# Transposing shifted attention scores by row halves of the PE array, and reordering the first token list of the routed MLP

## The chip, the cores and the metric

One core of one Trainium2 chip runs the kernel. The metric is the device time of one execution in microseconds (us); the kernel before took 655.96 us in the median of three runs (654.54 to 656.99).

## The reference

An attention with two kinds of local masks (heads 0 to 3: the last 32 keys; heads 4 to 7: every fourth of the last 128 keys) feeds a routed MLP with eight experts, in which every expert takes exactly `N // E` = 576 tokens, greedily by descending logit.

```python
q, k, v: (8, 8, 576, 64)   x: (4608, 512)   w1: (8, 512, 1024)   w2: (8, 1024, 512)
scores = scale * q @ k^T, masked;  attn = exp(scores - max) / (sum + 1e-9);  x = attn @ v
logits = x @ w_gate
for idx in argsort(-logits.flatten()):          # token idx // E, expert idx % E
    if assigned[tok] >= 0 or counts[e] >= cap: continue
    assigned[tok] = e; counts[e] += 1
for e: out[assigned == e] = relu(x[assigned == e] @ w1[e]) @ w2[e]
```

## The kernel before

The program has two stages, each with its own planner (class `Schedule`). The planner knows every operation's cost in ns, its dependencies and a boost to its due time; it simulates the engines and writes out a fixed order for each of them. An engine then executes its list in that order, whatever the real durations are. A matmul operation carries a form (how the PE array is divided); a change of form is planned at `T_TURN` = 95 ns.

**Attention.** There are 32 units (8 batches, two mask kinds, two head pairs of each kind). A unit handles two heads in nine blocks of 64 queries by 96 keys, ordered even blocks first (`ORD`, five even and four odd, `GR`). Its steps are: `scores` on PE (36 matmuls of 64x64 tiles of the array, form "quarter", into two PSUM banks `pm`); `most` on DVE (mask and row maximum, nine instructions); `shift` on POOL (subtract the maximum, one instruction for each of the two groups); `turn` on PE (nine transposes of [128 queries of two heads, 96 keys], form "whole", three to a PSUM bank `pS`, two banks in turn); `exps` on ACT (three instructions of 96x384); `values` on PE (36 matmuls, form "half", two groups into banks `px`); `sums` on ACT and `weigh` on DVE. After both head pairs of a kind, `banks` transposes the result on PE (nine transposes of 128x128, form "whole", three to a bank) and ACT copies it out; SP stores it to HBM (`xd`). Loads and stores share SP's queue in program order. `tokens` computes the gate logits, and `Router.choose` makes sort keys and the one-hot choice of each token on DVE (`keys`, `choices`).

**First list.** Between the stages, `Router.alone` runs with nothing beside it: a radix search over all keys (`search_alone`, PE and DVE in turn) finds the logit at which the first expert fills; then DVE finds which expert it is (`largest`, `expert`), its members (`members`), their ranks on PE (`ranks`), which of them are accepted (`need_of`, `accept`), their slots, digits and one-hot rows (`slots`, `digits`, `by_chunk` on POOL, `by_row` on ACT, `within` on DVE), and PE and DVE turn these into a list of row indices (`place`, `indices`). POOL gathers the tokens by that list with five indirect DMAs (`gather`).

**Experts.** Eight rounds of two matmul chains in split fp32r (high and low parts), while DVE searches for the next expert's list. `weights` casts the expert's weights on ACT (high part) and subtracts on DVE (low part).

PSUM is full: two banks `pm`, two `pS`, three `px` and one of the router.

## Time and profile before

| | us |
|---|---|
| median of three runs | 655.96 |
| the profiled execution | 656.71 |
| its span, first to last instruction | 654.7 |
| PE busy over the span | 619.2 (95%) |
| attention, to about | 158 |
| search of the first list, alone | 158 to 176 |
| first list and first gather | 176 to 193 |
| experts | 193 to 655 |

In a row of the profile a time is the start in us from the span's first instruction, followed by how long the instruction or the merged run of instructions took. Matmuls overlap, so the cost of one is read from start to start of the runs, not from its own duration. PEld is PE's weight load, SPq is SP's queue of DMA issues. A bracket at the end of a row is the idle time before it and what ended it.

### The profile page before, as it was taken

The page shows a single profiled execution, that of the slowest core. Times are in us where ns is not written, and L with a number is a line of the kernel's source. Part 1 is how long each engine was busy: PE and PEld are TensorE (multiplying, and loading weights), DVE is VectorE, ACT ScalarE, POOL GpSimd, SP SyncE. Part 2 cuts the span into 40 slices and gives each one's busy share as a digit, 9 for nine tenths or more (in the row PEclk, how much of TensorE's full clock was granted, in tenths as well). Part 3 has the DMA queues.
Part 4 walks back from the last instruction along what each step waited for, and adds up shares of the span by engine and source line. Part 5 has one row for each costly group of instructions (what it writes and reads, how often), then busy time and mean ns, then how long its engine had stood idle before and what let it go on. Part 6 is the DMA issues. An engine that isn't in the chain of part 4 may idle for free.

```text
span 654.7 us, 17735 instructions
## 1 busy us (share of the span) xinstructions
PE 619.2 (95%) x6635; PEld 534.3 (82%) x6636; DVE 454.1 (69%) x1916; ACT 306.9 (47%) x691; POOL 203.2 (31%) x322
## 2 busy tenths in 40 slices
PE   8999999997569999999999999999999999999994
PEld 5877788885439977987998898799889879989983
DVE  3768678875787888975897899689789927615200
ACT  3867788762038356742453434245344435324210
POOL 3434343330053167461025106202510621421011
PEclk9999999998579999999999999999999999999998
DMA  9999999623049379971154235115423643211010
GB/s 315 389 306 305 305 297 305 148 54 66 10 130 260 63 195 279 242 250 41 57 179 152 74 130 170 49 58 176 155 74 126 211 155 137 74 49 58 0 41 32
DMA packets 62646, 100.12 MB, mean 153 GB/s; under 512 B 7264, under 2 KB 26208, under 8 KB 62560
## 3 DMA queue, kind: packets, MB, share of 16 engines
q1 hardware_dynamic: 53216, 73.81, 34.6%
q0 software_dynamic: 9344, 25.17, 14.1%
q8 instruction: 52, 0.85, 0.5%
q14 instruction: 34, 0.28, 0.1%
HBM read 73.80 MB, written 18.87 MB: 142 GB/s over the span
## 4 chain that ended last, share of the span: by engine, by line
PE 70%; issue 12%; DVE 7%; POOL 4%; DMA 4%; ACT 1%; SPq 0%; POOLq 0%; DVEq 0%; ACTq 0%
PE ph L1207 26%; PE py L1249 17%; PE px L423 5%; PE pS L415 5%; PE pm L397 4%; PE px L474 2%; POOL xg L1155 2%; PE pz L657 2%; PE ptx L1170 2%; DMA xd<-xs 2%; POOL out L1275 2%; PE py L1252 1%; PE py L1254 1%; DVE ob L962 1%; PE pz L736 1%
## 5 line engine op out<-in xcount | busy, mean ns | idle before, releaser
L1249 PE MATMUL py<-w2h,hb 128*128 128x512 f32 x512 | 171.3, 399 | 0.0
L1207 PE MATMUL ph<-xh,w1h 128*128 128x256 f32 (+1 forms) x512 | 138.4, 301 | 0.7 <-ACT xh L1037 0.7
L1207 PE MATMUL ph<-xl,w1h 128*128 128x256 f32 (+1 forms) x512 | 136.3, 297 | 0.0
L1207 PE MATMUL ph<-xh,w1l 128*128 128x256 f32 (+1 forms) x512 | 136.2, 296 | 0.0
L1249 PEld LDWEIGHTS py<-w2h,hb 128*128 128x128 f32 x512 | 96.2, 188 | 18.9
L1037 ACT ACTIVATE hb<-ph 128x256 fp32r<-128x256 f32 (+2 forms) x192 | 59.8, 346 | 97.5 <-PE ph L1207 96.8
L1249 PE MATMUL py<-w2l,hb 128*128 128x512 f32 x256 | 100.0, 390 | 0.0
L1275 POOL DMA_INDIRECT out<-y,tok x40 | 41.0, 1025 | 169.0 <-ACT y L1037 95.8
L1207 PEld LDWEIGHTS ph<-xh,w1h 128*128 128x128 f32 x512 | 91.6, 190 | 1.4 <-ACT xh L1037 1.1
L1207 PEld LDWEIGHTS ph<-xh,w1l 128*128 128x128 f32 x512 | 91.6, 190 | 0.1
L1207 PEld LDWEIGHTS ph<-xl,w1h 128*128 128x128 f32 x512 | 91.4, 190 | 0.0
L408 POOL TENSOR_TENSOR sc<-sc,mx 128x480 f32<-128x480 f32 x64 | 56.9, 910 | 90.2 <-DVE mx L402 90.2
L1227 DVE SCALAR_TENSOR_TENSOR hb<-ph,hb 128x256 fp32r<-128x256 f32 (+1 forms) x128 | 57.3, 454 | 30.5 <-ACT hb L1037 28.7
L1037 ACT ACTIVATE y<-py 128x512 f32<-128x512 f32 (+1 forms) x40 | 23.9, 598 | 102.8 <-PE py L1249 95.4
L402 DVE CUSTOM_DVE_ANT_0 sc<-pm,const 128x96 f32<-128x96 f32 x288 | 53.8, 253 | 24.1 <-PE pm L397 24.0
L1155 POOL DMA_INDIRECT xg<-xd,idx x40 | 41.9, 1049 | 47.8 <-PE ph L1207 35.3
L1249 PEld LDWEIGHTS py<-w2l,hb 128*128 128x128 f32 x256 | 48.2, 188 | 8.4
L411 ACT ACTIVATE et<-pS 96x384 f32<-96x384 f32 x96 | 43.3, 485 | 23.9 <-PE pS L415 23.1
L1037 ACT ACTIVATE w1h<-raw 128x512 fp32r<-128x512 f32 x64 | 38.8, 629 | 28.1 <-DMA raw<-in_moe_w 27.2
L415 PE MATMUL pS<-const,sc 128*96 128x128 f32 x288 | 44.0, 281 | 1.0 <-ACT et L411 0.9
L1038 DVE TENSOR_TENSOR w2l<-raw,w2h 128x512 fp32r<-128x512 f32 x48 | 30.9, 685 | 19.1 <-ACT w2h L1037 18.8
L1037 ACT ACTIVATE xh<-ptx 128x512 fp32r<-128x512 f32 (+1 forms) x36 | 20.0, 555 | 51.4 <-PE ptx L1170 51.0
(170 smaller groups left out, 1024.4 us busy)
## 6 DMA issues: line engine op xcount, KB each, us to landing
raw<-in_moe_w SPq DMA_DIRECT2D x128, 256.0 KB, 5.1
k<-in_kp SPq DMA_DIRECT2D x16, 304.0 KB, 6.1
k<-in_kd SPq DMA_DIRECT2D x16, 304.0 KB, 6.4
q<-in_qp SPq DMA_DIRECT2D x16, 288.0 KB, 5.3
q<-in_qd SPq DMA_DIRECT2D x16, 288.0 KB, 6.2
xd<-xs SPq DMA_DIRECT2D x64, 72.0 KB, 2.9
xd<-xs SPq DMA_DIRECT2D x16, 288.0 KB, 6.2
w2l<-raw POOLq DMA_DIRECT2D x16, 256.0 KB, 5.5
```

Source lines behind the costliest of these rows:

```text
L402: nc.vector.tensor_tensor_reduce(out=sc[:, c], in0=pms[g][:, c // 2 * KB:c // 2 * KB + KB], in1=mm[:, c if self.kind else min(1, c)], scal ...
L408: nc.gpsimd.tensor_tensor(sc[:, g::2], sc[:, g::2], mx[:, g::2, None].to_broadcast([128, n, KB]), op=OP.subtract)
L411: nc.scalar.activation(self.E0[:, 384 * j:384 * j + 384], pt[:KB, :384], AF.Exp, scale=-1.0)
L415: nc.tensor.transpose(pt[:KB, 128 * x:128 * x + 128], sc[:, ORD[3 * j + x]], C["identf"])
L423: nc.tensor.matmul(px[64 * a:64 * a + 64, x - c0], self.E0[:, w:w + 64], self.V[c][a], start=True, stop=True)
L1037: act = lambda o, i, f=AF.Copy: nc.scalar.activation(o, i, f)
L1038: sub = lambda e, o, a, b: e.tensor_tensor(o, a, b, op=OP.subtract)
L1155: nc.gpsimd.indirect_dma_start(out=xg[:n], out_offset=None, in_=xd, in_offset=bass.IndirectOffsetOnAxis(ap=box[0][:n, m:m + 1], axis=0))
L1207: nc.tensor.matmul(o, a[:, d * 128:d * 128 + 128], b[:, d, c0:c1], start=((d, i) == pairs[0]), stop=((d, i) == pairs[-1]))
L1227: hl = op("DVE", 335 if j == 0 else 400, lambda: nc.vector.scalar_tensor_tensor(hb[:, CAP + c0:CAP + c1], o, 0.0, hb[:, c0:c1], op0=OP.max ...
L1249: nc.tensor.matmul(py, x, w, start=(f + i == 0), stop=(f == NF - 1 and i == 2))
L1275: s = nc.gpsimd.indirect_dma_start(out=out, out_offset=bass.IndirectOffsetOnAxis(ap=box[1][:n, m:m + 1], axis=0), in_=y[:n], in_offset=None)
```

## The change

In attention, a block's transpose is split by the rows of the array: queries 0 to 63 (one head) and 64 to 127 (the other head) are transposed by two matmuls of 64 rows each, with a 64x64 identity, into two different banks. `pS` becomes one buffer of two banks instead of two buffers of one bank. The nine blocks of a unit are transposed in two groups (five and four blocks) instead of three groups of three, `exps` has two instructions over both banks, and each group of `values` waits for its own group alone. The transposes have a form of their own, "rows".

In the first list, each token's chosen expert is kept as a power of two (`bits`, computed by `marks` in `choose`, and for the last batch within the search). The expert that fills is found as the power `wi`; membership is one bitwise and on DVE; the expert's number (`eidx`) and the set of open experts are computed on POOL; the count `need` is computed behind the start of `ranks`. `before` (the first half of `accept`) is split off. For the first list `by_chunk` moves from POOL to DVE, ahead of `within`; the first weight casts on ACT wait for `by_row`, and the first weight subtractions on DVE for the list. `first_gather` is a new indirect DMA of 16 rows on POOL at the start of the second stage, into a buffer that is not read.

```diff
+    f["pw"] = np.broadcast_to(2.0 ** (NE - 1 - np.arange(NE))[None, :], (128, NE)).astype(np.float32)
...
-    PM, PS, PV = Pool([banks_("pm", 2)]), Pool(banks_("pS", 2)), Pool(banks_("px", 3))
+    PM, PS, PV = Pool([banks_("pm", 2)]), Pool([ps.tile([128, 2, 512], F32, name="pS")]), Pool(banks_("px", 3))
+    def rows(out, in_):
+        for h in range(2):
+            p = slice(64 * h, 64 * h + 64)
+            nc.tensor.transpose(out[:, h], in_[p], C["identf"][p, p])
...
-            for j in range(3):
-                pt = Buf(PS)
-                t = self.op("PE", 330, lambda j=j, pt=pt: self.turn(j, pt.tile, sc), [*ex[:1 + (j > 0)], ready["c", 1]], B_T, pt)
+            for g, (c0, c1) in enumerate(GR):
+                n, pt = c1 - c0, Buf(PS)
+                t = self.op("PE", 62 * n, lambda c0=c0, c1=c1, pt=pt: self.turn(c0, c1, pt.tile, sc), [ex[g], ready["c", 1]],
+                            B_T, pt, "rows")
                 uses.append(t)
-                k = self.op("ACT", 400, lambda j=j, pt=pt: self.exps(j, pt.tile),
-                            [t, *olde], B_T)
+                k = self.op("ACT", 110 + 90 * n, lambda c0=c0, c1=c1, pt=pt: self.exps(c0, c1, pt.tile), [t, *olde], B_T)
...
-                            [*(et[:2] if g == 0 else et), *ready["V", kind, b, g], *(y for y in oldx if y.eng == "PE")],
+                            [et[g], *ready["V", kind, b, g], *(y for y in oldx if y.eng == "PE")],
...
-        def exps(self, j, pt):
-            nc.scalar.activation(self.E0[:, 384 * j:384 * j + 384], pt[:KB, :384], AF.Exp, scale=-1.0)
+        def exps(self, c0, c1, pt):
+            n = c1 - c0
+            e = self.E0[:, 128 * c0:128 * c1].rearrange("p (x h q) -> p h x q", x=n, h=2)
+            nc.scalar.activation(e, pt[:KB, :, :64 * n].rearrange("p h (x q) -> p h x q", x=n), AF.Exp, scale=-1.0)
-        def turn(self, j, pt, sc):
-            for x in range(3):
-                nc.tensor.transpose(pt[:KB, 128 * x:128 * x + 128], sc[:, ORD[3 * j + x]], C["identf"])
+        def turn(self, c0, c1, pt, sc):
+            for x in range(c0, c1):
+                rows(pt[:KB, :, 64 * (x - c0):64 * (x - c0) + 64], sc[:, ORD[x]])
...
+            if it == 2 and not last:
+                self.marks((B - 1) * S // 128, NCH)
...
+        if c1 < NCH:
+            self.marks(c0, c1)
+    def marks(self, c0, c1):
+        nc, b = self.tc.nc, self.bt[:, :c1 - c0]
+        nc.vector.tensor_tensor(b, self.oh0[:, c0:c1], self.C["pw"][:, None, :].to_broadcast([128, c1 - c0, NE]), op=OP.mult)
+            nc.vector.tensor_reduce(self.bits[:, c0:c1], b, axis=AX.X, op=OP.add)
...
+        fb = pw.tile([128, NE], F32, name="fb")
+        nc.vector.scalar_tensor_tensor(fb, self.pa[:, 1:1 + NE], self.delta, C["pw"], op0=OP.is_equal, op1=OP.mult)
...
+            nc.vector.tensor_reduce(wi, fb, axis=AX.X, op=OP.max)
+        nc.gpsimd.tensor_copy(ef, wi[:1])
+        nc.gpsimd.tensor_scalar(self.eidx, ef.bitcast(I32), -1.0 / 2 ** 23, float(126 + NE), op0=OP.mult, op1=OP.add)
...
+        nc.tensor.matmul(self.over, C["onesf"][:n], pr, start=True, stop=True)
         self.above()
+        nc.vector.tensor_tensor(te, self.bits, wi.to_broadcast([128, NCH]), op=OP.bitwise_and)
+        nc.vector.scalar_tensor_tensor(ge, te[:, None, :].to_broadcast([128, 2, NCH]), 0.0, self.gg, op0=OP.is_gt, op1=OP.mult)
+        self.ranks()
+        nc.vector.tensor_tensor(self.ohe, C["pw"], wi.to_broadcast([128, NE]), op=OP.is_equal)
+        nc.gpsimd.tensor_tensor(self.open, self.open, self.ohe, op=OP.subtract)
+        self.need_of()
+        self.before()
...
-        hi = op("ACT", 525, lambda: act(h, raw), [ld, *oldh], B_W)
+        hi = op("ACT", 525, lambda: act(h, raw), [ld, *oldh, st["row"] if n == "1" and r == 0 else None], B_W)
...
-            lo = op("DVE", 600, lambda: sub(nc.vector, l, raw, h), [ld, hi, *oldl], B_W)
+            lo = op("DVE", 600, lambda: sub(nc.vector, l, raw, h), [ld, hi, *oldl, st["ix"] if n == "1" and r == 0 else None], B_W)
...
-        x0 = op("POOL", 750, R.by_chunk, [d], B_L)
-        x1 = op("ACT", 490, R.by_row, [d], B_L)
+        x0 = op(*(("POOL", 750) if r else ("DVE", 440)), lambda: R.by_chunk(nc.gpsimd if r else nc.vector), [d], B_L)
+        first = [d] if r else [x0]
+        x1 = st["row"] = op("ACT", 490, R.by_row, [d], B_L)
...
+    def first_gather():
+        at = R.pw.tile([16, 1], I32, name="at", bufs=1)
+        nc.gpsimd.memset(at, 0)
+        nc.gpsimd.indirect_dma_start(out=row[:16], out_offset=None, in_=xd,
+                                     in_offset=bass.IndirectOffsetOnAxis(ap=at, axis=0))
+    row, _, use_row = Y.take()
+    use_row.append(op("POOL", 1200, first_gather, (), 1e6, lat=2500))
     round_(0)
```

## Rows read from the trace of the kernel before

**Rows 1.** The page: busy us of each engine, share of the span, instructions

```profile
PE 619.2 (95%) x6635; PEld 534.3 (82%) x6636; DVE 454.1 (69%) x1916; ACT 306.9 (47%) x691; POOL 203.2 (31%) x322
```

**Rows 2.** Windows: length, busy us (instructions) of each engine, granted clock, DMA share, GB/s

```profile
28.00:118.00 90.00, 86.54 (x1853) 72.09 (x1853) 65.12 (x468) 69.84 (x160) 33.95 (x39) 1.00 0.95 303
158.00:176.00 18.00, 10.73 (x310) 8.71 (x310) 11.52 (x57) 0.00 (x0) 0.00 (x0) 0.50 0.10 24
198.00:640.00 442.00, 441.16 (x3083) 391.08 (x3083) 313.75 (x1014) 189.17 (x425) 133.20 (x230) 1.00 0.41 127
```

**Rows 3.** Timeline of PE in steady attention: start, us, line, tiles, shape, count

```profile
113.97 0.84 PE L474 MATMUL px<-const,xs 128*128 128x128 f32 x6
114.64 0.49 PE L415 MATMUL pS<-const,sc 128*96 128x128 f32 x3
115.06 0.80 PE L423 MATMUL px<-v,et 96*64 96x65 f32 x20
115.80 0.86 PE L415 MATMUL pS<-const,sc 128*96 128x128 f32 x6
116.59 1.04 PE L397 MATMUL pm<-k,q 64*64 64x96 f32 x36
117.56 0.69 PE L423 MATMUL px<-vo,et 96*64 96x65 f32 x16
```

**Rows 4.** Timeline of PE's weight loads for the scores of the same unit

```profile
116.59 0.85 PEld L397 LDWEIGHTS pm<-k,q 64*64 64x64 f32 x36 [0.18 <-DMA xd<-xs]
```

**Rows 5.** Groups by shape, 0 to 160 us: busy us, mean ns, idle before

```profile
L411 ACT ACTIVATE et<-pS 96x384 f32<-96x384 f32 x96 | 43.3, 485 | 23.9 <-PE pS L415 23.1
L270 ACT ACTIVATE xt<-px 128x384 f32<-128x384 f32 x46 | 21.1, 488 | 5.2 <-PE px L474 5.1
L270 ACT ACTIVATE lt<-px 128x288 f32<-128x288 f32 x14 | 5.8, 411 | 3.2 <-PE px L515 2.4
```

**Rows 6.** Waits, 0 to 160 us: who waited for whom, us, times, longest

```profile
PEld pS L415 <- ACT et L411: 2.7, 6, 0.6
```

**Rows 7.** Timeline: the last load of values on SP, and its first use on PE

```profile
117.15 0.85 SPq L311 DMA_DIRECT2D v<-in_vd  x2
149.82 0.80 PE L423 MATMUL px<-v,et 96*64 96x65 f32 x20
```

**Rows 8.** Timeline of DVE from the expert found to the ranks read

```profile
176.76 0.21 DVE L852 TENSOR_SCALAR ohe<-fe,em 128x8 f32<-128x8 f32 x1
177.44 0.44 DVE L862 TENSOR_TENSOR pr<-oh,ohe 128x288 f32<-128x288 bf16 x1
178.40 0.23 DVE L866 TENSOR_TENSOR ge<-te,gg 128x72 bf16<-128x72 f32 x1
179.00 0.30 DVE L911 TENSOR_TENSOR_SCAN scan<-const,pz 128x72 f32<-128x72 f32 x1
```

**Rows 9.** Timeline of the first list: one-hot rows on DVE, by_chunk on POOL, indices

```profile
181.20 3.29 DVE L962 TENSOR_TENSOR ob<-si,const 128x768 bf16<-128x768 int32 x3
181.36 1.44 POOL L954 TENSOR_TENSOR rx<-oa,const 128x360 bf16<-128x360 bf16 x1 [33.12 <-DVE oa L949]
184.54 0.38 PE L969 MATMUL ptx<-rx,ob 128*128 128x40 bf16 x6 [0.49 <-DVE ob L962]
185.12 0.18 DVE L978 COPY t<-ptx 64x20 f32<-64x20 f32 x1
```

**Rows 10.** The line of `within`: duration ns min/median/max, first and last start us, shapes

```profile
L962 DVE TENSOR_TENSOR ob<-si,const x45: 539/547/1551, 181.2 to 558.2; 128x384 bf16<-128x384 int32 x42, 128x768 bf16<-128x768 int32 x3
```

**Rows 11.** Timeline: end of the indices, start of the gather, first and second list

```profile
185.53 0.33 DVE L981 SCALAR_TENSOR_TENSOR idx<-t 64x5 int32<-64x5 f32 x2
186.90 1.29 POOL L1155 DMA_INDIRECT xg<-xd,idx  x1 [4.10 <-DVE cap L894]
...
238.36 0.33 DVE L981 SCALAR_TENSOR_TENSOR idx<-t 64x5 int32<-64x5 f32 x2
238.97 1.44 POOL L1155 DMA_INDIRECT xg<-xd,idx  x1 [0.46 <-DVE idx L981]
```

More of the change, by code (lines that the diff above doesn't have):

```diff
@@ L629, in __init__ @@
         self.key0 = self.pf.tile([128, NCH], I32, name="key0")
+        self.bits = self.pf.tile([128, NCH], I32, name="bits")
+        self.bt = self.pf.tile([128, 5, NE], F32, name="bt")
         self.zero = self.pf.tile([128, 512], BF, name="zero")
@@ L775, in choose @@
         self.choices(c0, c1, self.M[:, sl], self.oh0[:, sl])
+        if c1 < NCH:
[3 more added lines that the diff above has]
+        nc.vector.tensor_tensor(b, self.oh0[:, c0:c1], self.C["pw"][:, None, :].to_broadcast([128, c1 - c0, NE]), op=OP.mult)
+        with nc.allow_low_precision(reason="sums of different powers of two under 256"):
+            nc.vector.tensor_reduce(self.bits[:, c0:c1], b, axis=AX.X, op=OP.add)
     def copies(self, oh, eng):
@@ L791, in alone @@
         self.search_alone(self.V2, self.oh, True)
-        nc, pw = self.tc.nc, self.pw
+        nc, pw, C = self.tc.nc, self.pw, self.C
         n = NK + 1
-        self.fe = pw.tile([128, NE], F32, name="fe")
-        nc.vector.scalar_tensor_tensor(self.fe, self.pa[:, 1:1 + NE], self.delta, self.C["pri"], op0=OP.is_equal, op1=OP.mult)
+        fb = pw.tile([128, NE], F32, name="fb")
+        nc.vector.scalar_tensor_tensor(fb, self.pa[:, 1:1 + NE], self.delta, C["pw"], op0=OP.is_equal, op1=OP.mult)
         s = pw.tile([n, 1], F32, name="sa")
-        nc.vector.tensor_scalar(s, self.C["kpos"][:n, 1:], self.delta[:n], None, op0=OP.is_equal)
-        em = self.largest()
+        nc.vector.tensor_scalar(s, C["kpos"][:n, 1:], self.delta[:n], None, op0=OP.is_equal)
+        wi = self.wi = pw.tile([128, 1], I32, name="wi")
+        with nc.allow_low_precision(reason="one of them, a power of two under 256"):
+            nc.vector.tensor_reduce(wi, fb, axis=AX.X, op=OP.max)
+        self.eidx = pw.tile([1, 1], I32, name="eidx", bufs=3)
+        ef = pw.tile([1, 1], F32, name="ef", bufs=1)
+        nc.gpsimd.tensor_copy(ef, wi[:1])
+        nc.gpsimd.tensor_scalar(self.eidx, ef.bitcast(I32), -1.0 / 2 ** 23, float(126 + NE), op0=OP.mult, op1=OP.add)
         pr = pw.tile([n, NE], F32, name="pra")
         nc.vector.tensor_scalar(pr, self.ps, s, None, op0=OP.mult)
-        self.expert(em)
+        self.over = self.pa[:, 16:16 + NE]
+        nc.tensor.matmul(self.over, C["onesf"][:n], pr, start=True, stop=True)
         self.above()
-        self.over = self.pa[:, 16:16 + NE]
-        nc.tensor.matmul(self.over, self.C["onesf"][:n], pr, start=True, stop=True)
+        te = pw.tile([128, NCH], I32, name="tb")
+        nc.vector.tensor_tensor(te, self.bits, wi.to_broadcast([128, NCH]), op=OP.bitwise_and)
+        ge = self.ge = pw.tile([128, 2, NCH], BF, name="ge")
+        nc.vector.scalar_tensor_tensor(ge, te[:, None, :].to_broadcast([128, 2, NCH]), 0.0, self.gg, op0=OP.is_gt, op1=OP.mult)
+        self.ranks()
+        self.ohe = pw.tile([128, NE], F32, name="ohe")
+        nc.vector.tensor_tensor(self.ohe, C["pw"], wi.to_broadcast([128, NE]), op=OP.is_equal)
+        nc.gpsimd.tensor_tensor(self.open, self.open, self.ohe, op=OP.subtract)
+        self.fe = pw.tile([128, NE], F32, name="fe")
+        self.need_of()
+        self.before()
     def low(self):
@@ L904, in ranks, with before @@
         nc.tensor.matmul(ps[:, 2 * NCH:], C["tri"], ge, start=True, stop=True)
-    def accept(self):
-        nc, C, pw, ge = self.tc.nc, self.C, self.pw, self.ge
+    def before(self):
+        nc, C, pw = self.tc.nc, self.C, self.pw
         ps = self.pz[:, 256:256 + 4 * NCH]
@@ L951, in digits, with by_chunk @@
         self.ob = pw.tile([128, NCH, 64], BF, name="ob", bufs=1)
-    def by_chunk(self):
-        self.tc.nc.gpsimd.tensor_tensor(self.rx[:, :, 0], self.oa,
+    def by_chunk(self, eng):
+        eng.tensor_tensor(self.rx[:, :, 0], self.oa,
                                         self.C["ctab"][:, :, None].to_broadcast([128, NCH, 2 * NM]), op=OP.mult)
@@ L1104, in settle @@
     def settle(r, e):
-        if r < NE - 1:
+        if r == 0:
+            rk = nd = None
+        elif r < NE - 1:
             m = chain("DVE", 1180, R.members, [e], B_L)
@@ L1112, in settle, with accept @@
             rk = chain("PE", 70, R.ranks, [nd], B_L)
-        ac = chain("DVE", 1000, R.accept, [rk, nd], B_L)
+        def accept():
+            if r:
+                R.before()
+            R.accept()
+        ac = chain("DVE", 1000 if r else 450, accept, [rk, nd], B_L)
         sl = st["slots"] = chain("DVE", 450, R.slots, [ac, st.get("digits")], B_L)
         ix, box = listing(r, sl)
+        st["ix"] = ix
         st["left"] = None
@@ L1134, in listing @@
             c0, c1 = c1, c1 + n
-            lows.append((op("DVE", 65 + 68 * n, lambda c0=c0, c1=c1: R.within(c0, c1), [d], B_L), c0, c1))
+            lows.append((op("DVE", 65 + 68 * n, lambda c0=c0, c1=c1: R.within(c0, c1), first, B_L), c0, c1))
         if r == 0:
```

6 lines of the change are left out of this document (4 added, 2 removed).

## The prediction

> **What bounds the kernel now.** I read the page first: PE is busy for 619.2 of 654.7 us [rows 1], so the question is which stretches PE sets and which it only waits through. The windows answer it [rows 2]. From 28 to 118 us PE is busy for 86.5 of 90 us, DVE for 65, ACT for 70. DMA's share is 0.95, close behind PE. From 198 to 640 PE is busy for 441.2 of 442. Between them, in the search, PE shows 10.7 of 18 us at a granted clock of 0.50 (1.2 GHz), and nothing but one chain of DVE and PE runs. So attention and the experts are bound by PE; the stretch from 158 to 193 us is bound by the length of its chain, and a us cut from that chain starts the experts a us earlier. A busy PE isn't PE at its peak, so attention is priced from start to start.
>
> **Transposes, the matmuls themselves.** Six transposes of 128x128 take 114.64 - 113.97 = 0.67 us, 0.112 each; three of `pS` with the change of form behind them take 115.06 - 114.64 = 0.42, so that a change costs 0.42 - 3 x 0.112 = 0.085 us; six of `pS` and a change take 0.79, the same within 0.03 [rows 3]. Nine blocks of a unit cost 9 x 0.112 = 1.01 us now. No row has a transpose on half the rows of the array. The nearest are the scores: 64x64 tiles, two row halves and two column halves at once, 36 of 96 columns in 117.56 - 116.59 = 0.97 us [rows 3]. Less a change of 0.09 that is 0.88, or 0.098 for a set of four. A pair of half transposes moves 64 columns instead of 96: 64/96 x 0.098 = 0.065. It loads two tiles of 96 columns, 192, where a set of four loads 4 x 64 = 256: 192/256 x 0.098 = 0.074. I take 0.070 a block, 0.63 a unit, which saves 0.38.
>
> The bounds: below, the pair could go at the spacing of the score matmuls, 0.024 each, 0.049 a block, which saves 0.57 a unit. Above, the two loads could go one behind the other. 36 loads of 64 columns are done in 0.85 us [rows 4]; values, with 64 columns on all 96 rows, take about 0.032 each (0.74 less a change, by 20) [rows 3], which scaled to 96 columns is 0.048, so 0.097 a block and a saving of 0.14 a unit.
>
> A rule of the Trainium skill speaks against this change. By "TensorE: Matmul & The Clock Gate", section "LDWEIGHTS (loading the stationary operand)", a weight load costs its columns over 1.2 GHz, whatever its rows; halving the rows then doubles the load work, and by this figure two loads of 96 columns one after the other would be an estimated 160 ns a block, 0.4 us a unit more than now. The scores' loads [rows 4] are spaced at 24 ns, where the rule gives 53 for 64 columns, so loads into different tiles do overlap here; whether two row halves under the same columns do is the one thing that they leave less sure.
>
> **Transposes, the changes of form.** The new form stands apart from that of the 128x128 transposes of `banks`, which now run beside `pS` without a change. A batch has six such pieces of three; two of them stand directly ahead of a run of `pS` [rows 3]. If all six stood alone between `pS` runs it would be 12 more changes, if the planner puts them together, with nothing of `pS` beside them, none; I take six of 0.09, 0.54 us a batch, 0.135 a unit. The net is 0.38 - 0.135 = 0.245 us a unit. In some 28 of 32 units PE sets the pace (the first two wait for loads, the last for their own chain): 28 x 0.245 = 6.9 us.
>
> **Exponentials.** ACT loses three instructions of 0.485 and gets two. By the copies of 384 and 288 columns, 0.488 and 0.411, a column costs 0.8 ns [rows 5]; 640 columns are 0.485 + 256 x 0.0008 = 0.69 and 512 are 0.59. ACT saves 0.18 us a unit, on an engine that isn't the bound: counted as nothing. That two banks and runs of 64 are read costs between 0 and 0.1 us an instruction; I take 0.
>
> **One buffer instead of two.** The second group's transposes now wait for the first group's exponential, and the next unit's first for the second's. Behind such a wait PE's whole list is queued. A turn of the buffer is 0.35 + 0.69 for five blocks and 0.28 + 0.59 for four, and four handovers between engines of some 0.15, together 2.5 us; a unit, added up from [rows 3], takes 0.97 + 1.01 + 1.34 + 0.5 for its half of `banks` and a few changes, some 4.1 us, and 3.9 after, so it fits if ACT comes promptly. In between PE needs some 0.9 us of other work twice a unit, and has scores (0.97) and values (0.74 and 0.6) for it [rows 3]. Today, with two buffers, PE's loads wait for this exponential for 2.7 us in all [rows 6]. I take 1 us more than the planner's order covers, with bounds of 0 and 12. In the last unit nothing covers: it ends some 0.4 us later. In the other direction the first `values` wait for one group and no longer for two; I take that as nothing. Attention's sum is 6.9 - 1 - 0.4 = 5.5, say 6 with what ACT's relief gives.
>
> **DMA behind it.** At a share of 0.95 DMA can't follow far [rows 2]: if 1.0 is all that it can do, four units of 4.1 us can't be fed in under 15.6. But loads lead: the last values are issued at 117 us and first used at 149.8 [rows 7], a lead of two batches that covers half a us a batch for all eight. No price here.
>
> **First list, members.** From the place of `ohe` at 176.76 to the ranks' `scan` at 179.00 DVE now does three small steps and two flags (to 177.44), product and sum over 288 columns and `ge` (from 178.40), and waits for PE [rows 8]. After the change the flags start at 176.76, the bitwise and over 36 columns follows at 177.05, `ge` at 177.28, and PE has its ranks at about 177.9 instead of 178.97. `ohe` and `need` then run on DVE beside PE, three dependent steps of 0.2, and hold `scan` until 178.0. The gain is 1.0 us, bounds 0.8 and 1.2. `marks` in attention adds two DVE instructions of 0.2 for each of seven batches, 2.8 us on an engine with 25 of 90 us to spare [rows 2]; for the last batch they stand where DVE waits for PE in the search: 0, or 0.3 if they come first. `eidx` goes to POOL, whose first instruction after a long rest may be slow; the first weights come up to 1 us later, but the first matmul that wants them is at 193 us, 12 us behind: 0.
>
> **First list, digits to gather.** `by_chunk` on DVE adds about 0.45 us (288 columns take 0.44 [rows 8]) ahead of `within`. But while POOL had it, 1.44 us long, the three `within` took 3.29 us [rows 9], and one of them 1.55 [rows 10]; the other two are then some 0.95 each. Without POOL beside them they should take 2.7: 0.6 back, 0.15 net, bounds -0.4 and 0.3. The weight subtraction that kept `indices` until 185.12, while PE was done at 184.92 [rows 9], goes behind the list: 0.12 more. Two or three subtractions of 0.68 then stand ahead of the second search, which has slack of under a us: -0.3, bounds -0.6 and 0.
>
> `first_gather` stands on POOL behind `eidx` and the update of the open set, at about 178, where POOL has no other work now that `by_chunk` is gone; if it ran into the list's gather it would cost 1 us. The first list's gather starts 1.04 us after its indices, the second list's 0.28 [rows 11], so a first use costs some 0.75 us, which the early one takes over: 0.75, bounds 0 and 0.75. The list's sum is 1.0 + 0.15 + 0.12 - 0.3 + 0.75 = 1.7 us, bounds 0.5 and 2.4. The experts' own work doesn't change.
>
> **Sum.** The profiled execution took 656.71 us, 654.7 of span and 2.0 around it; the median is 0.75 lower. 656.7 - 6 - 1.7 = 649.0 against the profiled one, 648.2 against the median, which I forecast.
>
> **The rivals.** (1) The pair costs its matmul spacing alone and the planner finds an order with few changes of form: 28 x 0.45 = 12.6, and 2 from the list, gives 641.5. For it speaks the 24 ns of the scores; against it that 96 columns are loaded and not 64. (2) The loads don't overlap: 0.14 a unit less 0.135 for changes, so attention stays as it is, and the list alone gives 654.3. [...] (3) Slower: the single buffer. If PE's list reaches the next group's transposes before ACT is through with the last one, PE stands still for up to 0.9 us; there are 64 such places. At 0.245 us a unit the gain is gone when 9 of the 64 are wholly uncovered (8 us); at 16 of 64 it is 14 us lost, 656 - 8 + 14 = 662. For it speaks that ACT is busy for 69.8 of 90 us [rows 2] with other copies between the exponentials in its list; against it the 2.7 us of today [rows 6]. (4) The change doesn't do what it says: the two halves load and run one behind the other, each at half of today's 0.112 to all of it [rows 3]. With the changes of form that is 28 x 0.135 = 4 us to 28 x (1.01 + 0.135) = 32 us more, less 1.7: 659 to 687, the near end the likelier. Against it, score tiles on the same columns and other rows run into different banks at once now [rows 3, 4]. This is the weight-load rule above, of the Trainium skill's "TensorE: Matmul & The Clock Gate"; its figure lies inside these ends, an estimated 16 us more and 671 in all.
>
> **How the numbers follow.** The forecast has 0.54 (645 to 652), rival 1 0.18, rival 2 0.14, rival 3 0.09 and rival 4 0.05. The likeliest time is 648.2; 642 to 655 takes in the forecast, rival 2 and most of rival 1. A measurement of this kernel can tell some 0.5% (3.3 us) from no change. Faster by more holds the forecast and rival 1 and a little of rival 2, 0.75; the same 0.14; slower 0.11.
>
> **What would show it.** Two matmuls of a block that start within 30 ns of each other and five blocks in about 0.35 us show the overlap; the six changes more a batch show as 128x128 transposes with a gap of 0.09 on both sides. PE's waits for `exps` should stay under 4 us in sum; more is rival 3. Attention should end near 152 instead of 158, `scan` follow the found expert 1 us sooner, and the first gather start under 0.4 us after its indices. I am wrong if a block takes 0.1 us or more, or if PE shows idle time ahead of `turn`.

## The result: slower by 1.1%, and the profile after

The changed kernel takes 662.15 us in the median of seven runs, the kernel before 655.81 beside it; the ratio is 1.0112, 95% interval [1.0089, 1.0135]. The profiled execution took 662.34 us with a span of 660.5, 5.8 more than before. The forecast of 648.2 and its range of 642 to 655 both missed.

Where the time went is found by milestones. First, the end of attention: the last gate matmuls, and the start of the first gather. The timeline of PE and of POOL, kernel before and then kernel after (start us, length us, line, tiles, shapes, count, idle before):

```profile
157.98 1.24 PE L539 MATMUL px<-wgp,xt 128*32 128x8 f32 x76 [0.37 <-ACT xt L270]
```

```profile
165.09 1.24 PE L549 MATMUL px<-wgp,xt 128*32 128x8 f32 x76 [0.37 <-ACT xt L278]
...
192.08 1.35 POOL L1208 DMA_INDIRECT xg<-xd,idx  x1 [5.02 <-DVE idx L1024]
```

Attention ends 7.1 us later. From there to the first gather it takes 27.0 us; before, with the gather of [rows 11], 28.9. So the list part gained 1.9 us, and attention lost 7.1 where a gain of 6 was forecast. From the gather to the end of the span it is 468.4 us against 467.8.

The page's busy time per engine, and the windows of steady attention, both after:

```profile
PE 617.4 (93%) x6925; PEld 529.2 (80%) x6928; DVE 456.8 (69%) x1930; ACT 305.4 (46%) x659; POOL 202.3 (31%) x326
```

```profile
28.00:118.00 90.00, 82.28 (x1967) 66.11 (x1968) 62.84 (x452) 65.07 (x132) 32.16 (x37) 0.98 0.97 301
```

In [rows 2] PE was busy for 86.5 of these 90 us, now for 82.3. PE has less work in each unit and stands more. The windows from 4 us to the start of the last `scores`, before and after, show how much:

```profile
4.00:144.13 140.13, 135.04 (x2853) 111.90 (x2853) 101.12 (x738) 102.69 (x235) 54.24 (x61) 1.00 0.87 277
4.00:151.29 147.29, 131.95 (x3166) 106.41 (x3168) 103.47 (x752) 103.50 (x209) 55.17 (x62) 0.99 0.85 264
```

PE is busy for 3.1 us less and idle for 15.3 us instead of 5.1. The transposes themselves did what the diff says. The timeline of PE after, in steady attention:

```profile
127.05 0.48 PE L276 MATMUL pS<-const,sc 64*96 64x64 f32 x10
127.47 1.04 PE L405 MATMUL pm<-k,q 64*64 64x96 f32 x36
128.49 0.43 PE L276 MATMUL pS<-const,sc 64*96 64x64 f32 x8
128.84 0.80 PE L433 MATMUL px<-v,et 96*64 96x65 f32 x20
```

Five blocks take 0.42 us from start to start and four 0.35, the change of form included; before, six took 0.79 and three 0.42 [rows 3]. But PE waits more in attention, and above all at `turn` (who waited for whom, 4 to 158 us: us, times, longest). Rows of each, first before, then after:

```profile
PE pm L397 <- issue: 1.7, 2, 0.9
PE px L423 <- issue: 1.1, 1, 1.1
PE pS L415 <- ACT et L411: 0.9, 3, 0.4
```

```profile
PE pS L276 <- issue: 4.8, 4, 2.2
PE pm L405 <- issue: 2.3, 4, 1.2
PE pS L276 <- ACT et L421: 1.9, 4, 1.0
PE px L433 <- issue: 1.3, 2, 0.9
PE pS L276 <- POOL sc L416: 1.2, 1, 1.2
```

"Issue" is a stop of PE's matmuls that waits for nothing the profile shows. Such stops make 8.4 us in attention now, 2.7 before. The waits for other engines and for loads, added up to the start of the last `scores`, are 7.0 us now and 2.1 before: for exponentials 1.9, for DVE's row maxima 1.3, for POOL 1.2, the rest smaller. What follows takes the change apart to find which of its parts costs the time, and what these stops are.

### The profile page after: what moved, and what is told of

It reads as the page before. It is cut to its first block, busy times and chain, and to the rows that moved or that the text cites. A ratio compares the mean times of both kernels' runs of the same rounds, so it can differ in the third digit from the quotient of the medians.

```text
span 660.5 us, 18299 instructions
## 1 busy us (share of the span) xinstructions
PE 617.4 (93%) x6925; PEld 529.2 (80%) x6928; DVE 456.8 (69%) x1930; ACT 305.4 (46%) x659; POOL 202.3 (31%) x326
## 4 chain that ended last, share of the span: by engine, by line
PE 53%; issue 11%; DVE 6%; POOL 2%; DMA 1%; ACT 1%; POOLq 0%; SPq 0%; DVEq 0%; ACTq 0%
PE ph L1260 24%; PE py L1302 19%; PE pz L669 2%; PE ptx L1223 2%; DMA raw<-in_moe_w 1%; POOL out L1328 1%; PE py L1305 1%; PE py L1307 1%; PE pz L748 1%; PE ph L119 1%; DVE G L683 1%; DVE ob L1005 1%; PE ptx L1012 1%; POOL xg L1208 0%; DVE hb L1280 0%
## 5 line engine op out<-in xcount | busy, mean ns | idle before, releaser
L1302 PEld LDWEIGHTS py<-w2h,hb 128*128 128x128 f32 x512 | 96.2, 188 | 19.2
L421 ACT ACTIVATE et<-pS 96x640 f32<-96x640 f32 x64 | 41.3, 645 | 28.4 <-PE pS L276 27.8
L1081 DVE TENSOR_TENSOR xl<-ptx,xh 128x512 fp32r<-128x512 f32 (+1 forms) x36 | 22.9, 635 | 25.0 <-ACT xh L1080 25.0
```

Of the source, the lines that this page charges most:

```text
L421: nc.scalar.activation(e, pt[:KB, :, :64 * n].rearrange("p h (x q) -> p h x q", x=n), AF.Exp, scale=-1.0)
L1081: sub = lambda e, o, a, b: e.tensor_tensor(o, a, b, op=OP.subtract)
L1302: nc.tensor.matmul(py, x, w, start=(f + i == 0), stop=(f == NF - 1 and i == 2))
```

## The experiments

Ratios are to the kernel before on the same chip, with 95% intervals.

**The two parts apart.** The list part, and the attention part, each alone: the other part's lines of the diff taken back.

> The kernel before with the first list's part of the change alone; attention's order is untouched. Every theory expects attention to end where it ended before (last gate matmuls of the last batch at 157.98 us) and the list to give back what the changed kernel shows there: from the end of attention to the first gather 28.9 us before, 27.0 after, so 1.5 to 2.3 us faster than before, about 654.

> The kernel before with attention's part of the change alone. If the two parts add up: 7 to 9 us slower than before, since the list no longer takes 2 us off; attention ends near 165 us. If instead the list's part (its extra instructions for bits in every batch on DVE, or another placing of constants) upset attention, attention ends under 160 and this kernel is within 2 us of before.

The list part gave 1.000 [0.9975, 1.0026], the attention part 1.012 [1.0055, 1.0184]. The loss is attention's alone. The list's 1.9 us (0.997) don't show in this ratio, though they lie inside its interval. Nor did attention end near 158 us in the profile of the list part, as expected, but at 161.65, with a stop of 1.8 us and the granted clock at 0.96 over 28 to 118 us; attention's order is the old one there. So a milestone of one execution can be some 4 us off.

**The one buffer without the row halves.** Whole transposes into one buffer of two banks, in groups of five and four, each group of `values` behind its own group, as in the change; `exps` has three instructions, of four blocks, one and four. Shown against the attention part alone:

```diff
-                rows(pt[:KB, :, 64 * (x - c0):64 * (x - c0) + 64], sc[:, ORD[x]])
+                k, m = (x - c0) % 2, (x - c0) // 2
+                nc.tensor.transpose(pt[:KB, k, 128 * m:128 * m + 128], sc[:, ORD[x]], C["identf"])
```

> Attention's part with one buffer of two banks and groups of five and four, but with whole transposes of 128x128, nine matmuls a unit as before, in the old form; the group of five has two exponentials. Theory A (PE's instructions come too late: the row halves add 576 instructions to PE's list, and it stands still at regular distances in it, while DMA is full): this kernel has as few PE instructions as before, so PE's stops without a visible cause stay at the 2.8 us of before (8.4 after) and the time is within 3 us of before. Theory B (the single buffer: PE's list waits for the exponential): this kernel has the same buffer and dearer transposes, so it is at least as slow as the rows kernel, 8 to 14 us over before, with waits of PE's transposes for the exponential of over 5 us.

Measured 1.0084 [1.0055, 1.0113], 5.5 us (3.6 to 7.5), between the times of both theories: the buffer, with the grouping that it brings, costs by itself most of the attention part's 7.9 us on this chip. In its profile, of the fastest of its seven executions, the stops that wait for nothing are only 0.4 us and attention ends at 158.09 us. So the buffer's cost and the stops are different things, and this profile doesn't show where the 5.5 us lie.

**Without most loads.** The loads of q and k are left out from the third batch on, in the row halves and in the kernel before; a plain run of the kernel before stands beside them.

```diff
-nc.sync.dma_start(t[kind][s][:, part], src[b][:, part])
+nc.sync.dma_start(t[kind][s][:, part], src[b][:, part]) if b < 2 else None
```

> The kernel before once more, for a profile on the same chip as the next three. Attention should end at 157 to 160 us; the experts should last as long as in the next three runs.

> Attention's part alone, in the same planned order, with the loads of q and k left out from batch 2 on (the tiles of two batches earlier are used again, so the result is not the reference's). DMA then moves about half the bytes from 35 to 115 us. Theory A (PE's instructions come late because DMA is full): PE's stops without a visible cause fall from 8 us to under 2, and against the next kernel the row halves cost at most 3 us, or gain. Theory B (the buffer and the changes of form): those stops matter little, and it stays 5 to 8 us slower than the next kernel.

> The kernel before with the same loads left out from batch 2 on. Theory A: its own stops without a visible cause, 2.8 us, go to under 1, so 1 to 3 us faster than before. Theory B, and any theory in which DMA has no part: within 1 us of before.

The kernel before again took 656.5 us in its one run. Without the loads the row halves gave 0.9956 [0.9927, 0.9985] and the kernel before 0.9957 [0.9927, 0.9988]. The loss of 1.2% is gone, and no gain stands in its place: 654.07 against 653.72 us in the medians, on one chip. The stops fall to 1.0 us in the row halves and to 0 in the kernel before.

**Marks in attention or in the search.** The list part alone, with `bits` made in six pieces in the search instead of batch by batch in attention, first on one chip, then beside the other form on another:

```diff
-            if it == 2 and not last:
-                self.marks((B - 1) * S // 128, NCH)
+            if self.marked < NCH:
+                self.marks(self.marked, self.marked + 6)
+                self.marked += 6
```

> The list's part alone, with the bits of all batches computed in six pieces of six chunks within the search, where DVE waits for PE, and none in attention. If the 14 small DVE instructions that the bits add to attention are what ate the list's gain in the list-only run (ratio 1.000 where 0.997 was expected): attention ends where before's does and it is 1.2 to 2.4 us faster than before, ratio 0.9965 to 0.998. If they cost nothing and the list's gain is lost elsewhere: ratio 0.999 to 1.002.

> The list part alone, with the marks in attention as the change has them: the kernel that gave 1.000 [0.9975, 1.0026], beside the one with the marks in six pieces in the search, which gave 0.9953 on another chip. Theory A (the two marks instructions of each batch hold up attention): attention ends 2 us later here than in the next run and the ratio stays near 1.000, 0.003 or more above it. Theory B (the marks cost nothing, as the prediction has it, and the difference was one of chips): both give about 0.9965, and both end attention within 0.5 us of the kernel before.

> The list part alone, with no marks in attention and six pieces of six chunks in the search. Both theories: 0.994 to 0.998; the list's gain of 1.9 us is 0.997 by itself, and anything below that is attention's. It is the reference for the run before this one on the same chip.

Late marks gave 0.9953 [0.9928, 0.9978] on the first chip. Side by side on the next, with the same two kernels, early marks gave 0.9985 [0.9952, 1.0019] and late ones 0.9988 [0.9956, 1.0019]. Both ended attention at 156.9 us in their profiles. So the marks cost nothing that can be measured, as predicted, and the difference of the first two list runs was one of chips. The list part with late marks is the only version that came out ahead of the kernel before wherever it ran, by 0.1% and 0.5%; it is shown as faster on one of its two chips.

**More instructions, nothing else.** The row halves add 288 matmuls and 288 weight loads. The kernel before with nine one-column matmuls more in each unit, with and without the loads:

```diff
+                w = 64 * (c % 2)
+                nc.tensor.matmul(o[w:w + 64, :1], self.Q[c][:64], self.K[c][:64, :1], start=True, stop=True)
```

> The kernel before, whole transposes and two single-bank buffers, with nothing added but nine one-column score matmuls a unit, each ahead of the block that overwrites it: 9 loads and 9 matmuls, as many instructions as the row halves add, 576 in all. Theory A (PE's instruction supply behind a full DMA stops it): stops of PE that wait for nothing visible rise from 2 to 3 us to 6 or more, at whole multiples of some 251 instructions of its list, and the time is 7 us (the work itself, at 24 ns a pair) and 4 to 6 us more: 1.015 to 1.02. Theory B (the count of instructions doesn't matter, the row form or the one buffer makes the stops): stops stay at 2 to 3 us and the time is at most the added work, 1.000 to 1.011.

> The same nine one-column matmuls a unit, with the loads of q and k left out from the third batch on (the scores then go by old data; order and all else as they are). Without the added matmuls this gave 0.9957. Theory A: with DMA relieved the stops stay under 1.5 us, and the time holds the added work alone, 0.9957 plus up to 0.011. Theory B: the same time, and the run before this one is dearer than this one by no more than the 0.004 that the loads cost the kernel before.

They gave 1.0263 [1.0175, 1.035] and 1.0226 [1.016, 1.0292], both over the expected times. The page of the first has:

```profile
PE 642.3 (94%) x7210; PEld 556.4 (82%) x7212; DVE 455.1 (67%) x1916; ACT 307.9 (45%) x691; POOL 199.6 (29%) x322
```

That is 575 matmuls and 576 loads more than before [rows 1], twice what the row halves add and twice what was expected: a call of this kind, like the 18 of a unit's scores, runs as two matmuls and two loads. A unit's scores with them take 65.39 - 63.84 = 1.55 us from start to start against 0.97 [rows 3], 0.58 us for 18 pairs of a load and a matmul, or 0.03 a pair where 0.024 had been taken. The loads of q and k cost 0.0037 here, no more than they cost the kernel before, but the intervals are wider than that. The stops are 2.9 us with twice the added instructions. The theory that the number of instructions suffices falls. The test has a limit: PE is slower here, and DMA's share over 28 to 118 us was 0.89 instead of 0.95.

**Row halves in two buffers.** The two banks are cut across, so that a buffer is half of both; three groups of three blocks, as before:

```diff
-    PM, PS, PV = Pool([banks_("pm", 2)]), Pool([ps.tile([128, 2, 512], F32, name="pS")]), Pool(banks_("px", 3))
+    halves = lambda t: [t[:, :, :256], t[:, :, 256:]]
+    PM, PS, PV = Pool([banks_("pm", 2)]), Pool(halves(ps.tile([128, 2, 512], F32, name="pS"))), Pool(banks_("px", 3))
```

The second of these runs is the same kernel again, without the list part, whatever its label says.

> Attention part alone, by row halves, but the two banks of pS are cut into two buffers, each half of both banks, with three groups of three blocks and three exponentials as before: the row form with two buffers. Theory A (the one buffer makes the loss: groups wait for exponentials, and PE then runs in bursts): the loss of 1.2% goes, 0.994 to 0.999, PE's stops that wait for nothing visible stay under 4 us, and its waits for exponentials near 1 us. Theory B (the row form with its 576 added instructions and its changes of form makes it, behind a full DMA): 1.007 to 1.015, stops of 6 us or more. If both share it: 1.000 to 1.006.

> The kernel of the run before once more, for a second profile: stops that stand at the same places of PE's list are the kernel's own and not chance. Theories A and B as there.

> The row halves in two half-bank buffers, with the loads of q and k left out from the third batch on (scores by old data). The row halves in one buffer gave 0.9956 so, the kernel before 0.9957. Theory A (one buffer makes the loss): 0.990 to 0.994, since the transposes' gain is no longer eaten by waits for the one buffer. Theory B (the row form makes it): 0.9956 or above, since changes of form eat the gain whatever the buffers.

> Whole transposes in one buffer of two banks, groups of five and four, with the loads of q and k left out from the third batch on (scores by old data). With the loads it gave 1.0084. Theory A (waits for the one buffer, of themselves): 1.003 to 1.005, as much above the kernel before without loads (0.9957) as with them. Theory C (the one buffer only hurts behind a full DMA): 0.995 to 0.998.

Measured, with the earlier runs in their places:

| | with loads | without loads of q, k | last `scores` start, without loads (us) |
|---|---|---|---|
| whole, two buffers (before) | 1 | 0.9957 [0.9927, 0.9988] | 141.17 |
| whole, one buffer | 1.0084 [1.0055, 1.0113] | 1.0028 [0.9997, 1.0059] | 143.92 |
| row halves, two buffers | 1.0015 [0.9972, 1.0058] | 0.995 [0.9924, 0.9977] | 139.84 |
| row halves, one buffer (the change) | 1.012 [1.0055, 1.0184] | 0.9956 [0.9927, 0.9985] | 142.50 |

The rows are from three chips, and one kernel, that with the late marks, gave ratios 0.0035 apart on two chips, so differences between rows are rough. With loads the one buffer costs 5.5 us under whole transposes and 6.9 under row halves (0.0105 of 656, by the intervals some 5 us either way); without loads 0.0071 and 0.0006. With two buffers the row halves can't be told from the kernel before in the same column. So by the time with loads both theories share the loss, and without loads the row halves in two buffers lie between the two; the one buffer under whole transposes, 1.0028, is just under what its waits alone were to give. The last column is the start of the last unit's scores in the timeline of PE, one execution each:

```profile
141.17 1.04 PE L397 MATMUL pm<-k,q 64*64 64x96 f32 x36
```

```profile
143.92 1.04 PE L404 MATMUL pm<-k,q 64*64 64x96 f32 x36
```

```profile
139.84 1.04 PE L405 MATMUL pm<-k,q 64*64 64x96 f32 x36
```

```profile
142.50 1.04 PE L404 MATMUL pm<-k,q 64*64 64x96 f32 x36
```

(In the order of the table.) By these starts one buffer is 2.7 us later under either form, and row halves 1.3 to 1.4 us earlier with either pool. But the executions differ in more than the lists. The windows from 4 us to these starts, of the kernel before and of the row halves in two buffers, both without loads of q and k:

```profile
4.00:141.17 137.17, 134.62 (x2853) 111.44 (x2853) 100.84 (x738) 102.62 (x235) 54.30 (x61) 1.00 0.64 177
4.00:139.84 135.84, 126.17 (x3124) 103.39 (x3125) 98.66 (x738) 101.47 (x235) 55.12 (x62) 0.97 0.64 179
```

Of the four, only the row halves in two buffers ran at a lower granted clock for a while, 0.90 from 20 to 30 us and 0.76 from 30 to 40, behind a stop of 0.92 us. Stop and clock are worth up to 4.3 us, an estimate from these windows; without them the row halves would be 5 to 6 us earlier with two buffers, and the one buffer would cost all of that. The medians (0.995 against 0.9957) show no such gain. So how the two effects add up stays open. The windows show another thing: PE is busy for 8.5 us less, yet idle for 9.7 us instead of 2.6. Without the stops, PE's waits add up to 8.6 us in the row halves with two buffers and 5.8 with one, 4.6 in the whole transposes with one buffer and 2.2 in the kernel before. With faster transposes PE waits for the other engines. The waits of matmuls for `exps` alone, 0 to 160 us with loads, are 4.8 and 3.7 us in two profiles of the row halves with two buffers, where 1 us was expected, 2.7 after the change, 2.2 in the whole transposes with one buffer and 0.9 before; so the row halves bring more of them than the single buffer does.

With loads the gain is lost: in the two profiles of the two-buffer kernel, the second of which is the "list" label, the gate matmuls that end attention start at 164.18 and at 157.93 us, in the two of the kernel before at 157.98 and at 155.74. Windows of the two, first the one that was late (length, busy us and instructions of PE, PEld, DVE, ACT, POOL, granted clock, DMA share, GB/s):

```profile
28.00:60.00 32.00, 28.58 (x634) 23.41 (x634) 20.08 (x143) 22.57 (x53) 11.65 (x14) 0.89 0.97 301
90.00:118.00 28.00, 25.61 (x624) 21.07 (x621) 20.14 (x154) 20.62 (x48) 10.82 (x13) 0.94 0.90 276
```

```profile
28.00:60.00 32.00, 29.33 (x707) 23.50 (x706) 22.33 (x168) 24.83 (x56) 12.82 (x15) 1.00 0.95 296
90.00:118.00 28.00, 25.15 (x626) 19.96 (x626) 20.93 (x148) 19.55 (x47) 11.67 (x13) 1.00 0.98 324
```

One program, one order of work: the first ran 634 matmuls where the second ran 707, at a granted clock of 0.89 instead of 1.00. Its stops that wait for nothing were 7.5 us against 4.7.

**What the stops are.** They came at like distances in every profile. Counted from the head of the list, the numbers of PE's visible matmuls and weight loads ahead of two stops differ by about 251 or a multiple of it. To tell the fetching of the list from the work that stands there, the head of the list is made 124 instructions longer:

```diff
-    keep_clock(nc, warm, fill, F0)
+    keep_clock(nc, warm, fill, F0 - 1)
+    for _ in range(63):
+        nc.tensor.matmul(fill[:32, :8], warm[:, :32], warm[:, :8], start=True, stop=True)
```

> The attention part alone as in the second run (row halves, one buffer), with one warm-up matmul fewer and 63 tiny matmuls (32 by 8) ahead of the first scores, where PE waits for its loads anyway: 124 instructions more at the head of PE's list. There the stops stood behind 937, 1692, 1944, 2699, 3201, 3452 and 4207 visible instructions. Theory A (the list is fetched in pieces of some 251 instructions, behind other transfers): stops stand at the same counts of the list or at whole multiples of 251 from them, so 124 instructions earlier in the work. Theory B (the work at that place makes them): they stand 124 higher, at 1061, 1816, 2068, 2823, 3325, 3576 and 4331.

The stops in the timeline of PE at four counts at which both kernels stopped, with the windows from 0 to just before the first and the last; first the attention part alone, then the shifted one (the first two counts of a window are PE's and PEld's):

```profile
0.00:27.40 27.40, 21.43 (x467) 15.68 (x470) 15.19 (x126) 15.43 (x27) 10.75 (x20) 1.00 0.96 344
28.07 0.26 PE L275 MATMUL pS<-const,sc 64*96 64x64 f32 x2 [1.31 <-issue]
51.72 0.48 PE L404 MATMUL pm<-k,q 64*64 64x96 f32 x12 [0.84 <-issue]
86.21 0.71 PE L404 MATMUL pm<-k,q 64*64 64x96 f32 x20 [0.43 <-issue]
0.00:121.33 121.33, 107.68 (x2480) 84.95 (x2482) 79.12 (x589) 83.01 (x164) 45.08 (x58) 0.97 0.94 305
121.74 0.45 PE L432 MATMUL px<-vo,et 96*64 96x65 f32 x8 [0.81 <-issue]
```

```profile
0.00:25.63 25.63, 21.03 (x468) 15.88 (x471) 12.88 (x106) 13.48 (x23) 9.44 (x18) 1.00 0.95 340
26.07 0.79 PE L404 MATMUL pm<-k,q 64*64 64x96 f32 x25 [0.87 <-issue]
48.81 0.34 PE L556 MATMUL px<-const,lt 128*64 128x8 f32 x5 [0.33 <-issue]
86.44 0.28 PE L432 MATMUL px<-v,et 96*64 96x65 f32 x2 [0.43 <-issue]
0.00:117.88 117.88, 108.01 (x2480) 86.08 (x2484) 76.71 (x568) 80.70 (x159) 43.24 (x56) 0.96 0.94 310
118.13 0.40 PE L556 MATMUL px<-const,lt 128*64 128x8 f32 x7 [0.49 <-issue]
```

The counts are 937, 1944, 3452 and 4962 in the one, 939, 1945, 3454 and 4964 in the other; what stands behind them differs each time: transposes and scores, scores and gate matmuls, scores and values, values and gate matmuls. The remaining stops of the shifted kernel stand at 1190 and 2448, one and six times 251 above 939, but for one of 0.34 us at 7.41 us, in the warm-up. None stands 124 higher. So the stops belong to places in the list and not to the work: PE waits for the next piece of its own list. The page's DMA queue "q8 instruction" moves as many packets as that makes (packets, MB, share), before, after, and with the one-column matmuls:

```profile
q8 instruction: 52, 0.85, 0.5%
```

```profile
q8 instruction: 54, 0.88, 0.5%
```

```profile
q8 instruction: 57, 0.93, 0.6%
```

Before, PE and PEld have 13271 instructions [rows 1], 255 for each of 52 packets; after, 6925 + 6928 by 54 is 257; with the one-column matmuls, 7210 + 7212 by 57 is 253.

The trace has the packets too. In all profiles of this document there are 69 stops of this kind in attention behind the first packet, and each of them ended 1.2 to 1.7 us after a 16 KB packet of this queue had ended. The longest after the change, and the row of the queue in the window from 95.2 to 96.2 us:

```profile
97.70 0.37 PE L276 MATMUL pS<-const,sc 64*96 64x64 f32 x6 [2.25 <-issue]
q8 instruction: 1, 0.02, 5.5%
```

The packet ran from 95.22 to 96.10 us, and PE went on at 97.70. With the loads of q and k gone the stops nearly go, and the packets come earlier in the list: all nine packets behind which PE stopped in the attention part alone began 26 to 210 instructions further on in PE's list than the same packets without those loads. The sixth began when PE had started 1656 instructions with the loads, and 1500 without. So the loads delay the pieces; how they do isn't seen.

**The change with its buffer mended.**

> The whole change with the buffer mended: row halves in two half-bank buffers (1.0015 alone) and the list part with the marks in the search (0.9953 and 0.9988 alone on two chips). By the sum of both: 0.996 to 1.001, and not faster than the list part alone. If the row halves gained 6.9 us with two buffers, as the prediction priced them, it would be 0.987.

Measured 1.0039 [1.0016, 1.0062], above the upper end of the sum, 1.001. The row halves don't pay here in either pool.

## Why the prediction was wrong, step by step

**The price of a block: right, a little better.** 0.070 us was taken; in the run of ten matmuls at 127.05 us the two of a block start 3 ns apart and the blocks follow each other every 0.055 us. The two halves do overlap, and rivals 2 and 4 fall. The weight-load rule of the Trainium skill, "TensorE: Matmul & The Clock Gate", section "LDWEIGHTS (loading the stationary operand)", would give an estimated 0.16 us a block if the halves loaded in turn; the trace has 0.055, so these don't.

**The changes of form: more of them, and dearer.** Six more a batch is 48, at 0.09 us. From 4 to 148 us, by the forms that the planner gives its operations, PE's timeline has 128 changes in the kernel before without loads and 196 in the row halves without loads, 68 more. The start-to-start distances of its runs, less what their matmuls take undisturbed and without the stops over 0.2 us, sum to some 11.2 and 20.2 us: 9.0 by 68 is 0.13 us a change. With two buffers it is 47 more changes for some 5.2 us, 0.11. In the rows above a run of five blocks takes 0.42 - 5 x 0.055 = 0.14 us beyond its blocks, and three whole transposes 0.085 [rows 3]. The term was 4.3 us and is some 9. Against 288 blocks that save 0.112 - 0.055 each, 16.4 us, some half of the gain goes here, in a form that stands beside none of its neighbours'.

**The single buffer: mis-sized.** 1 us was taken, with bounds of 0 and 12; it is 5.5 us under whole transposes, and under row halves 6.9 with loads and 0.4 without, by the intervals some 5 and 3 us either way. The step looked for the cost in PE's waits for `exps`, and those stay small: the matmuls' are 2.7 us after and 0.9 before (the 2.7 of [rows 6] are those of the weight loads), so the test set for rival 3 (over 4 us) doesn't fire. Under whole transposes and without loads the last scores start 2.75 us later with one buffer, and PE's waits for `exps` rise only from 0.9 to 2.2 us. The list that the planner writes for one buffer has changed too, with 12 changes of form more, 1 us at 0.09. That such a list gives the time up in its order is inferred, and how the 5.5 us divide wasn't settled. Rival 3 gave the right time (662) by luck: of its 14 us of bare waits for `exps` at 16 of 64 places the trace shows PE's waits for all engines and loads 4.9 us longer, and 1.3 of these are for `exps`.

**"PE sets the pace" in 28 of 32 units: not any more.** The forecast turned all of PE's saving in these units into time. The windows above have PE idle for 15.3 us instead of 5.1 up to the last scores; without the stops it is 7.0 us of waits instead of 2.1. The sign that was set for this, idle time of PE ahead of `turn`, is there: 4.8 us for its list, 1.9 for `exps` and 1.2 for POOL.

**"DMA behind it: no price": the step that failed most.** The windows [rows 2] gave DMA 0.95 of the bound stretch, and the lead of [rows 7] seemed cover enough. The loads of data had that lead; the pieces of PE's list, which share the 16 DMA engines, came too late. Without the loads of q and k the attention part costs nothing, with them 1.2%. In the profiled executions the stops account for 8.4 - 2.7 = 5.7 us of the 7.1. The clock follows. The timeline of PE after, and the windows that hold this stop and come behind it:

```profile
28.58 0.34 PE L276 MATMUL pS<-const,sc 64*96 64x64 f32 x2 [1.56 <-issue]
28.86 1.35 PE L433 MATMUL px<-v,et 96*64 96x65 f32 x20
30.14 1.86 PE L405 MATMUL pm<-k,q 64*64 64x96 f32 x36
```

```profile
20.00:30.00 10.00, 7.74 (x157) 6.20 (x153) 5.54 (x43) 6.04 (x12) 3.55 (x4) 0.93 1.05 398
30.00:40.00 10.00, 10.00 (x236) 8.34 (x236) 7.23 (x61) 7.96 (x16) 3.87 (x5) 0.90 0.94 261
```

Behind the stop of 1.56 us the granted clock falls, and 20 values take 1.28 us from start to start instead of 0.74 [rows 3]; 0.93 and 0.90 of two windows of 10 us are up to 1.7 us more. Why the row halves meet more stops isn't shown. DMA's share alone doesn't tell: over 28 to 118 us it is 0.94 both in the attention part alone, with 8.0 us of stops, and in the whole transposes with one buffer, with 0.4.

**Exponentials: right.** 0.69 and 0.59 us were forecast for five and four blocks. The groups by shape, 0 to 160 us, after:

```profile
L421 ACT ACTIVATE et<-pS 96x640 f32<-96x640 f32 x32 | 22.4, 699 | 16.1 <-PE pS L276 16.0
L421 ACT ACTIVATE et<-pS 96x512 f32<-96x512 f32 x32 | 18.9, 592 | 12.2 <-PE pS L276 11.9
```

**The list: right in its sum and in most of its terms.** 1.7 us were forecast, 1.9 came. The timeline of DVE, PE and POOL after:

```profile
183.65 0.15 DVE L823 TENSOR_REDUCE wi<-fb 128x1 int32<-128x8 f32 x1
185.10 0.29 DVE L950 TENSOR_TENSOR_SCAN scan<-const,pz 128x72 f32<-128x72 f32 x1
186.00 1.07 POOL L1357 DMA_INDIRECT y<-xd,at  x1 [0.96 <-POOL at L1356]
187.89 2.69 DVE L1005 TENSOR_TENSOR ob<-si,const 128x768 bf16<-128x768 int32 x3
191.47 0.33 DVE L1024 SCALAR_TENSOR_TENSOR idx<-t 64x5 int32<-64x5 f32 x2
```

From the found expert to `scan` it is 1.45 us instead of the 2.49 from its predecessor `em`: 1.04, forecast 1.0. `within` takes 2.69 instead of 3.29 [rows 9] without POOL beside it, 0.60 back, forecast 0.6, for 0.53 of `by_chunk` ahead of it, forecast 0.45. The gather stands 0.28 us behind its indices instead of 1.04 [rows 11]: `first_gather` took over the 0.76.

In sum: 1.7 of the list held, and the block's saving was better than its estimate. What turned 6 us of gain into a loss of 7.1, some 13 us, can be read from the two profiles up to the last scores. The stops for PE's own list are 5.7 of them and the clock behind a stop up to 1.7, both priced at nothing. PE's other waits grew by 4.9 where 1.4 had been allowed. PE's own work fell by some 4.8, the slower clock taken out, instead of 6.9. The single buffer is no term beside these; what it costs lies within the waits and the work.

## What to carry to other kernels

Measure a scarcer buffer alone, before the gain that it pays for: it cost 5.5 us here while PE's waits for it stayed small. Count the changes of form that a new form adds, since here they took back half of what the faster transposes saved. Ask which engine sets the pace once PE is faster. And where DMA runs near full beside a bound TensorE, look at the stops that wait for nothing: TensorE's own list comes by the same DMA engines, and here the loss went when the stops went.

## What the runs showed of the hardware

PE's instruction list arrives in packets of 16 KB (0.85 MB by 52), one for 253 to 257 visible instructions. Beside the loads of q and k a packet can come so late that PE stands still, for up to 2.5 us (2.53 in the kernel with the one-column matmuls), until 1.2 to 1.7 us after the packet's end. Between 4 and 150 us of these profiles the granted clock fell to 0.50 (1.2 GHz) eleven times, each time during such a stop or less than 3 us behind one; behind most of the 69 stops it didn't fall. Two 64-row transposes of 96 columns run side by side at 0.055 us a pair, and a run of them takes some 0.14 us beyond its pairs. A 64x64 load with a matmul of one column, put among the scores, costs 0.03 us. An indirect DMA that is the first on POOL starts 0.76 us later than one that isn't.
